# Attention pairs 0 to 12 on 64-row TensorE tiles, in a new order, with q and k stacked and one division for both heads

## The chip, the cores and the metric

The kernel runs on one core of a Trainium2 chip. The core has a matrix engine (TensorE, PE), whose results land in PSUM, a memory of eight banks; VectorE (DVE), ScalarE (ACT) and GpSimd (POOL), which compute on PSUM and on SBUF, the working memory of 128 partitions; and SyncE (SP), which issues transfers. Each engine takes its own instructions in the order in which they are written and waits for others by semaphores. The metric is device time in microseconds, the median of several runs. Smaller is better.

## The reference

Attention with a bias that depends on the distance of two positions, for 8 batches of 8 heads of 576 positions and 64 channels; then a layer of two matrix products with a leaky rectifier between them.

```python
scores = scale * np.matmul(q, k.transpose(0, 1, 3, 2))
bias = bias_table[bucket]                  # bucket from |i - j|; one value for |i - j| >= 128
scores = scores + bias.transpose(2, 0, 1)[None, :, :, :]
attn = np.exp(scores - np.max(scores, axis=-1, keepdims=True))
attn = attn / (np.sum(attn, axis=-1, keepdims=True) + 1e-09)
x = np.matmul(attn, v)                     # heads side by side: (4608, 512)
h = x @ w_in                               # (512, 2048)
out = np.maximum(0.01 * h, h) @ w_out      # (2048, 512)
```

## The kernel before

The work is 32 pairs of heads (`items`: batch b, pair p, numbered n = 4b + p), interleaved with pieces of the layer. All matrix operands are bf16.

**A pair.** Its rows of q and k come from DRAM in blocks that lie on `RQ` = 96 partitions, six positions to a partition (`load_qk`, L119; tiles `qn`, `kn`). They have to be turned, so that the 64 channels of each of the two heads lie on partitions: `turned_pair` (L280) does it on TensorE for pairs 0 to 8, by identity products into PSUM tiles `ps_t` (for pairs 0 to 5 straight from the loaded rows, 12 of them for q and 12 for k; for 6 to 8 from rows that `pair_rows`, L265, has put side by side on VectorE, 6 and 6). From pair 9 on a DMA transpose (`turn_by_dma`, L276) does it. Copies then bring q and k into `qt` and `kt` (`copy_q`, `copy_k`). Scores (`qk_mm`, L333) have keys on partitions: four blocks u of 128 keys for the first 512 queries, both heads in one buffer `ps_s` of two banks; u = 4 is the last 64 queries against the four blocks; u = 5 is the last 64 keys of both heads, laid over 128 rows with zeros between (`apart`, L297). `exp` (L370) is the exponential on ScalarE into `at`, `at4`; `band` (L387) multiplies the near-diagonal part by the exponential of the bias (`hk`) on VectorE. The value products add to two banks `ps_o`, one for each head: `av_tails` (L412) for the last keys, then `av_chunks` (L425), `av` or `av_phase` (L465) for the four blocks; a 65th column of ones gives the row sums. `divide` (L447) takes a reciprocal and a product for each head, into `opair`, which is turned once more into `xT`, the layer's input: on TensorE (`x_turn`, L484) or by DMA (`x_transposes`).

**The layer.** For each of nine blocks T of 512 tokens there are 16 "in" pieces (four products of 512 columns into one bank `pm`, then a leaky rectifier on ScalarE, `leaky`, into `gt`) and four "out" pieces of 16 products each, copied to `y` and stored. Block 0 needs all four pairs of batch 0, block 1 those of batches 0 and 1.

**Tile height.** A product may use all 128 rows of TensorE, or 64: two with different halves of the rows then run at the same time. Scores use 64 rows a head (L354). Before, the value products of pairs 0 to 6 (`av_chunks`, L432) and of pair 31 (`av`, L442) use 128 rows, and so do most layer pieces ahead of pair 13 (L532, L584); the rest of that stretch goes by halves of the rows (L476, L720). From pair 13 on (`body_in_lanes`, L915) everything goes in two 64-row lanes (`lanes`, L849): each layer piece is done in two halves, and two pieces run side by side. Two halves must not add to the same bank at the same time; where that could come about, `hold` (L460) puts an empty TensorE instruction that waits for the end of a given product.

**What sets the order.** Pairs 0 to 7 follow a list written out by hand (`first`, L1115; `m n u` is a score, `e` its exponential, `b` a bias product, `at` and `ac` value products, `dv` a division, `i`, `p0`, `p1`, `moe` and `o` layer pieces). Pairs 8 to 12 follow a loop (L1213) with a plan of layer pieces (`plan`, `body_in_halves`, L739); pairs 13 to 31 `body_in_lanes`; then `moe_rest` (L1023). PSUM is split into two `ps_s` buffers of two banks, two single banks `ps_o`, and two single banks that `ps_t`, `ps_tx` and `pm` share. GpSimd issues the loads in the order of `load_qk`, `load_v_part` and `spread_loads` (L1075); SP the stores and DMA transposes.

Of the kernel before, what the change touches and what calls it, by code (L numbers as in the profile page):

```python
# [37 lines left out]
def kernel(  # L38
# [10 lines left out]
    nc = tc.nc  # L49
# [23 lines left out]
    op_pool = ctx.enter_context(tc.tile_pool(name="op", bufs=2))  # L73
# [20 lines left out]
    RQ = 96  # L94
    NC = S // RQ
    qn = [per.tile([P, H, NC, D], BF16, name=f"qn{i}") for i in range(NBUF)]
    kn = [per.tile([P, H, NC, D], BF16, name=f"kn{i}") for i in range(NBUF)]
# [21 lines left out]
    def load_qk(b, h0, h1, which=("q", "k")):  # L119
        i = b % NBUF  # L120
        for name, src, dst in (("q", q, qn[i]), ("k", k, kn[i])):
            if name not in which:
                continue
            nc.gpsimd.dma_start(
                out=dst[0:RQ, h0:h1, :, :].rearrange("r h c d -> r h (c d)"),
                in_=src[b, h0:h1, :, :].rearrange("h (r c) d -> r h (c d)", c=NC),
            )
# [148 lines left out]
    def turn_by_dma(n):  # L276
        t = turned[n] = tu_pool.tile([P, 2 * NC, RQ], BF16, name="tu")
        nc.sync.dma_start_transpose(out=t, in_=prs.pop(n).rearrange("r j c d -> r (j c d)"))

    def turned_pair(n, j):  # L280

        if by_dma(n):
            return turned[n][:, j * NC : (j + 1) * NC, :].rearrange("p c r -> p r c")
        ps = ps_m_pool.tile([P, 8 * P], BF16, name="ps_t", tag="m")
        b, p = items[n]
        for c in range(NC):
            if n > n_pairs + 1:
                nc.tensor.transpose(ps[:, c * RQ : (c + 1) * RQ], in_=prs[n][:, j, c, :],
                                    identity=ident[0:RQ, 0:RQ])
                continue  # L290
            for e in range(2):
                nc.tensor.transpose(ps[e * D : (e + 1) * D, c * RQ : (c + 1) * RQ],  # L292
                                    in_=(qn, kn)[j][b % NBUF][0:RQ, 2 * p + e, c, :],
                                    identity=ident[0:RQ, 0:RQ])
# [1040 lines left out]
```

## Time and profile before

| what | value |
|---|---|
| median of 3 runs | 364.85 us (364.39 to 365.44) |
| profiled execution, first to last instruction (its span) | 362.8 us |
| TensorE busy in it | 353.4 us (97%) |
| VectorE busy | 189.5 us (52%) |
| ScalarE busy | 243.4 us (67%) |
| GpSimd busy | 107.4 us (30%) |
| mean granted TensorE clock | 0.995 |

The profile is one execution. It gives no time of its own for what lies around the span; the median of the runs is 2.1 us over the span. An engine's busy time is the union of its instructions. A row of the timeline gives start, length, engine, source line, operation, `out<-in`, the tile of TensorE (rows*columns), shapes and a count; a length over several instructions runs from the first start to the last end, and products overlap, since each lasts longer than the distance to the next. What stands in brackets at a row's end is idle time before it and what ended it.

### The profile page before, as it was taken

The page shows a single profiled execution, that of the slowest core. Times are in us where ns is not written, and L with a number is a line of the kernel's source. Part 1 is how long each engine was busy: PE and PEld are TensorE (multiplying, and loading weights), DVE is VectorE, ACT ScalarE, POOL GpSimd, SP SyncE. Part 2 cuts the span into 40 slices and gives each one's busy share as a digit, 9 for nine tenths or more (in the row PEclk, how much of TensorE's full clock was granted, in tenths as well). Part 3 has the DMA queues.
Part 4 walks back from the last instruction along what each step waited for, and adds up shares of the span by engine and source line. Part 5 has one row for each costly group of instructions (what it writes and reads, how often), then busy time and mean ns, then how long its engine had stood idle before and what let it go on. Part 6 is the DMA issues. An engine that isn't in the chain of part 4 may idle for free.

```text
span 362.8 us, 12074 instructions
## 1 busy us (share of the span) xinstructions
PE 353.4 (97%) x5174; PEld 204.7 (56%) x5191; DVE 189.5 (52%) x499; ACT 243.4 (67%) x364; POOL 107.4 (30%) x195
## 2 busy tenths in 40 slices
PE   7899999999999999999999999999999999999996
PEld 3465555555556777666666665565666544444443
DVE  3796876677756767655555566556554300200000
ACT  5999888479958898777777777777776264054111
POOL 8857617254334344432243334211000000000000
PEclk8999999999999999999999999999999999999999
DMA  8999999997899899979998889875111000210212
GB/s 104 196 193 147 190 206 159 197 156 115 99 130 137 114 148 139 138 120 122 133 136 124 108 119 129 122 103 96 52 49 51 29 31 0 85 33 0 80 66 87
DMA packets 106429, 40.27 MB, mean 111 GB/s; under 512 B 83713, under 2 KB 102409, under 8 KB 106377
## 3 DMA queue, kind: packets, MB, share of 16 engines
q0 software_dynamic: 55200, 18.36, 48.4%
q1 hardware_dynamic: 49880, 19.06, 27.2%
q10 hardware_dynamic: 1296, 2.10, 1.6%
q8 instruction: 41, 0.67, 0.7%
q14 instruction: 12, 0.09, 0.1%
HBM read 37.68 MB, written 9.45 MB: 130 GB/s over the span
## 4 chain that ended last, share of the span: by engine, by line
PE 93%; DVE 3%; ACT 1%; issue 1%; DMA 1%; POOL 0%; ACTq 0%; POOLq 0%
PE pm L845 35%; PE pm L584 16%; PE pm L532 15%; PE ps_o L476 8%; PE ps_s L354 8%; PE pm L720 2%; PE ps_o L432 2%; PE ps_o L421 1%; PE ps_s L845 1%; DMA kn<-in_k_dram 1%; DVE at L408 1%; PE ps_t L292 1%; PE pm L577 1%; PE ps_s L347 1%; PE ps_s L357 1%
## 5 line engine op out<-in xcount | busy, mean ns | idle before, releaser
L845 PE MATMUL pm<-xT,w_in_sb 64*128 64x512 bf16 x608 | 142.1, 376 | 0.0
L373 ACT ACTIVATE at<-ps_s 128x1024 bf16<-128x1024 f32 x120 | 118.6, 1026 | 33.7 <-PE ps_s L354 32.1
L845 PE MATMUL pm<-w_out_sb,gt 64*128 64x512 bf16 x544 | 132.6, 376 | 0.0
L556 ACT ACTIVATE gt<-pm 128x512 bf16<-128x512 f32 x140 | 82.1, 605 | 38.8 <-PE pm L532 33.4
L408 DVE TENSOR_TENSOR at<-at,hk 128x768 bf16<-128x768 bf16 (+3 forms) x149 | 65.6, 453 | 41.6 <-ACT at L385 24.8
L845 PEld LDWEIGHTS <-w_in_sb 64*128 64x128 bf16 x608 | 50.7, 94 | 20.4 <-issue 0.7
L845 PEld LDWEIGHTS <-gt 64*128 64x128 bf16 x544 | 47.0, 94 | 22.7 <-issue 3.5
L584 PE MATMUL pm<-w_out_sb,gt 128*128 128x512 bf16 x261 | 59.0, 379 | 0.7 <-issue 0.5
L532 PE MATMUL pm<-xT,w_in_sb 128*128 128x512 bf16 x242 | 56.9, 379 | 0.5
L354 PE MATMUL ps_s<-qt,kt 64*128 64x512 bf16 x240 | 44.3, 383 | 2.3 <-ACT at L373 0.8
L584 PEld LDWEIGHTS <-gt 128*128 128x128 bf16 x268 | 25.5, 98 | 29.9
L532 PEld LDWEIGHTS <-w_in_sb 128*128 128x128 bf16 x252 | 23.7, 98 | 27.0 <-issue 0.6
L476 PE MATMUL ps_o<-vn,at 64*128 64x65 bf16 x1920 | 38.4, 190 | 0.0
L476 PEld LDWEIGHTS <-at 64*128 64x128 bf16 x1920 | 35.7, 94 | 4.6 <-issue 4.4
L131 POOL DMA_DIRECT2D vn<-in_v_dram x32 | 33.8, 1060 | 9.1 <-issue 4.2
L385 ACT ACTIVATE at<-ps_s 128x576 bf16<-128x576 f32 x30 | 19.9, 663 | 17.9 <-PE pm L845 17.9
L454 DVE TENSOR_TENSOR opair<-ps_o,rcp 128x320 bf16<-128x320 f32 x64 | 29.1, 487 | 1.1
L896 DVE COPY y<-pm 128x512 f32<-128x512 f32 x17 | 11.8, 692 | 27.7 <-PE pm L845 27.7
L597 DVE COPY y<-pm 128x512 f32<-128x512 f32 x11 | 7.6, 691 | 33.5 <-PE pm L584 30.6
L354 PEld LDWEIGHTS <-kt 64*128 64x128 bf16 x240 | 14.7, 94 | 16.7 <-issue 6.6
L1088 POOL COPY tick<-opair 1x1 bf16<-1x1 bf16 x43 | 7.9, 185 | 54.6 <-DVE opair L454 54.6
L1088 POOL COPY tick<-at 1x1 bf16<-1x1 bf16 x21 | 5.5, 263 | 61.0 <-DVE at L408 61.0
(108 smaller groups left out, 348.9 us busy)
## 6 DMA issues: line engine op xcount, KB each, us to landing
out_dram<-y SPq DMA_DIRECT2D x24, 256.0 KB, 3.7
qn<-in_q_dram POOLq DMA_DIRECT2D x28, 144.0 KB, 4.7
kn<-in_k_dram POOLq DMA_DIRECT2D x28, 144.0 KB, 3.5
vn<-in_v_dram POOLq DMA_DIRECT2D x24, 128.0 KB, 4.5
w_in_sb<-in_moe_w_in_dram POOLq DMA_DIRECT2D x4, 512.0 KB, 9.2
w_out_sb<-in_moe_w_out_dram POOLq DMA_DIRECT2D x2, 1024.0 KB, 13.4
out_dram<-y ACTq DMA_DIRECT2D x7, 256.0 KB, 2.0
vn<-in_v_dram POOLq DMA_DIRECT2D x16, 64.0 KB, 8.0
```

The source lines that it names most:

```text
L131: nc.gpsimd.dma_start(out=vn[b % NBUF][:, c, h0:h1, 0:D], in_=v[b, h0:h1, c * P : (c + 1) * P, :].rearrange("h s d -> s h d"),)
L354: nc.tensor.matmul(ps[:, e, :], lhsT=kt[r, u * P : (u + 1) * P], rhs=qt[r, 0:512], start=True, stop=True)
L373: nc.scalar.activation(at[:, :, u, 0:512], ps, AF.Exp, scale=scale)
L385: nc.scalar.activation(at4[:, 0:w], ps.rearrange("p e i -> p (e i)")[:, 0:w], AF.Exp, scale=scale)
L408: nc.vector.tensor_tensor(out=o, in0=o, in1=m, op=ALU.mult)
L454: nc.vector.tensor_tensor(out=opair[:, 0:m, e * D : (e + 1) * D], in0=ps[:, :, 0:D], in1=rcp.to_broadcast([P, m, D]), op=ALU.mult)
L476: m = nc.tensor.matmul(outs[n][e][:, ic * (D + 1) : (ic + 1) * (D + 1)], lhsT=at[halves[r], o : o + P], rhs=vn[b % NBUF][halves[r], c, 2 * ...
L532: nc.tensor.matmul(pm, lhsT=w_in_sb[:, c, f * P : (f + 1) * P], rhs=xT[c][:, T * TT : (T + 1) * TT], start=(c == 0), stop=(c == n_cc - 1))
L556: nc.scalar.activation(g, pm, AF.Prelu, bias=0.0, scale=1.0, alpha=0.01)
L584: nc.tensor.matmul(pm, lhsT=gt[:, f, ts * P : (ts + 1) * P], rhs=w_out_sb[:, f, :], start=(f == 0), stop=(f == n_fc - 1))
L845: m = nc.tensor.matmul(o, lhsT=w, rhs=x, start=was is None, stop=need[bank] == 0)
L1088: nc.gpsimd.tensor_copy(out=tick, in_=at4_[home(n)][0:1, S - 1 : S] if part == 2 else ops_[n - 2 + part][0:1, 0, 0:1])
```

## The change

Five things are changed together.

1. `RQ` is 64. q lies on partitions 0 to 63 and k on 64 to 127 of one tile `qkn`, nine positions to a partition. `pair_rows` makes one copy for both, the DMA transpose turns nine blocks of 128 rows instead of twelve of 96, and `turn_by_pe` turns q and k with 64-column products on the two halves of the rows. Pair 9 keeps the DMA, pairs 0 to 8 TensorE.
2. The value products of all pairs go in two lanes (`value_steps`), as do the last-key scores (`Tails`: two half-width products of each lane) and the output transposes (`x_turn`, two halves); the layer pieces of the first part come as `Duo`, two pieces side by side.
3. `ps_o` is one buffer of two banks. `divide` makes one reciprocal and one product for both heads. A `Duo` in a two-bank buffer is closed by one rectifier of 1024 columns.
4. A new list orders pairs 0 to 12 (before: 0 to 7, then the loop). The planner and `body_in_halves` are gone; pairs 13 to 31 keep `body_in_lanes`, where two pieces `i2`, `i3` now share the `ps_o` buffer, and the next pair's first score comes behind the last pieces. The three warming products (`warm`) are gone.
5. The last pair's value products are woven with four layer pieces; `moe_rest` follows with five banks in turn instead of six.

```diff
-    RQ = 96
+    RQ = P // 2
...
+    qkn = [per.tile([P, H, NC, D], BF16, name=f"qkn{i}") for i in range(NBUF)]
+    rows_of = {"q": slice(0, RQ), "k": slice(RQ, P)}
...
-        t = prs[n] = pr_pool.tile([RQ, 2, NC, 2 * D], BF16, name="pr")
-        for j, src in enumerate((qn, kn)):
-            nc.vector.tensor_copy(out=t[:, j, :, :].rearrange("r c (e d) -> r c e d", e=2),
-                                  in_=src[b % NBUF][0:RQ, 2 * p : 2 * p + 2, :, :].rearrange("r e c d -> r c e d"))
+        t = prs[n] = pr_pool.tile([P, NC, 2 * D], BF16, name="pr")
+        nc.vector.tensor_copy(out=t.rearrange("r c (e d) -> r c e d", e=2),
+                              in_=qkn[b % NBUF][:, 2 * p : 2 * p + 2, :, :].rearrange("r e c d -> r c e d"))
...
+    def turn_by_pe(n, which):
...
+        for c in range(NC):
+            for j in which:
+                r = halves[j]
+                o = ps[j][:, c * RQ : (c + 1) * RQ]
+                if rows is not None:
+                    nc.tensor.transpose(o, in_=rows[r, c, :], identity=ident[r, r])
+                    continue
+                for e in range(2):
+                    nc.tensor.transpose(o[e * D : (e + 1) * D, :], in_=qkn[b % NBUF][r, 2 * p + e, c, :],
+                                        identity=ident[r, r])
...
+            for e in range(2):
+                need[id(ps), e] = 2
+                t.append(((id(ps), e), ps[:, e, 0:w], kt[:, S : S + P], qt[:, e * w : (e + 1) * w]))
+            self.todo = [[t[0], t[1]], [t[1], t[0]]]
...
+    def divide(n):
+        ops_[n] = op_pool.tile([P, NJ + 1, 2 * D], BF16, name="opair")
+        of = outs.pop(n)[:, :, 0 : (NJ + 1) * (D + 1)].rearrange("p e (i d) -> p e i d", d=D + 1)
+        rcp = rc_pool.tile([P, 2, NJ + 1, 1], FP32, name="rcp")
+        nc.vector.reciprocal(rcp, of[:, :, :, D : D + 1])
+        nc.vector.tensor_tensor(out=ops_[n].rearrange("p i (e d) -> p e i d", e=2), in0=of[:, :, :, 0:D],
+                                in1=rcp.to_broadcast([P, 2, NJ + 1, D]), op=ALU.mult)
...
+        def go(self, i, k):
+            a, b = self.p
+            if i:
+                a, b = b, a
+            lanes(a.take(0, k), b.take(1, k))
...
+                nc.scalar.activation(g, self.both, AF.Prelu, bias=0.0, scale=1.0, alpha=0.01)
...
-        i2, i3 = Piece("in", ps_o_pool, "o0"), Piece("in", ps_o_pool, "o1")
+        i23 = Duo("in", "o")
+        i2, i3 = i23.p
...
+            lanes(i2.take(0, 4) + i3.take(0, 4), two.take(1, 8))
+            i23.close()
+            lanes(i4.take(0, 4), two.take(1, 4))
+            i4.close()
+            two.close(True)
             if nxt:
                 score(n + 1, 0)
-            for i in (i2, i3, i4):
-                lanes(i.take(0, 4), two.take(1, 4))
-                i.close()
-            two.close(True)
             return
...
-            chunks = {(n_pairs + 2, 2): (0,), (n_pairs + 3, 1): (1, 2, 3)}.get((n, part), ())
+        if n <= 3 * n_pairs:
+            chunks = {(6, 2): (0, 1, 2, 3), (9, 1): (0, 1), (10, 1): (2, 3)}.get((n, part), ())
...
-        ac 3 1 3, e 4 2, p0 0,
-        begin 4, m 4 3, dv 3 0.1, e 4 3, xt 3 o0, xc 3, b 4 0, p0 1, p1 0 0, p1 1 0, m 4 4 s, b 4 1, m 4 5,
+        l t5 0 1 t5 1 1, x1 2, l t5 0 1 t5 1 1, xc 2 v, x0 3, e 5 5, m 5 0, b 4 1, x1 3, e 5 0, m 5 2, xc 3 v,
+        b 5 5, sl 5 2, in f0F1 m, d f0F1 0 2, b 4 5, e 5 2, at 4, b 5 0, m 5 4, d f0F1 0 2, e 5 4, m 4 4, b 5 2,
```

The order of the engines is best seen where the layer begins. On TensorE, before, its first products (`pm`, three of piece 0) stand ahead of pair 4's score of block 3 and pair 3's output transposes:

```order
L532 LDWEIGHTS w_in_sb
L532 MATMUL pm_791<-xT_94,w_in_sb 128x512
L532 LDWEIGHTS w_in_sb
L532 MATMUL pm_791<-xT_95,w_in_sb 128x512
L532 LDWEIGHTS w_in_sb
L532 MATMUL pm_791<-xT_96,w_in_sb 128x512
L354 LDWEIGHTS kt_111
L354 MATMUL ps_s<-qt_118,kt_111 128x512
L354 LDWEIGHTS kt_111
L354 MATMUL ps_s<-qt_118,kt_111 128x512
L490 LDWEIGHTS opair
L490 MATMUL ps_tx<-ident,opair 128x128
```

In the changed kernel they come behind pair 5's score of block 2 (L341), two pieces (`pm_1094`, `pm_1096`) in turn on the two halves:

```order
L341 LDWEIGHTS gt
L341 MATMUL ps_s<-gt 128x512
L341 LDWEIGHTS gt
L341 MATMUL ps_s<-gt 128x512
L406 LDWEIGHTS w_in_sb
L406 MATMUL pm_1094<-xT_94,w_in_sb 128x512
L406 LDWEIGHTS w_in_sb
L406 MATMUL pm_1096<-xT_94,w_in_sb 128x512
L406 LDWEIGHTS w_in_sb
L406 MATMUL pm_1094<-xT_95,w_in_sb 128x512
L406 LDWEIGHTS w_in_sb
L406 MATMUL pm_1096<-xT_95,w_in_sb 128x512
```

The start of the layer has moved from ahead of a score of pair 4 to behind one of pair 5, and 128-row and 64-row products no longer alternate.

On ScalarE, before, the last rows ahead of the first rectifier (L556) are pair 3's and pair 4's exponentials and two copies of turned q (L307):

```order
L373 ACTIVATE at_112<-ps_s 128x2x512 x3
L307 COPY qt_118<-ps_t 128x576
L385 ACTIVATE at_0_114<-ps_s 128x576
L375 ACTIVATE at_112<-ps_s 128x8x64
L307 COPY gt<-ps_t 128x576
L373 ACTIVATE at_113<-ps_s 128x2x512 x4
L556 ACTIVATE gt<-pm_791 128x512
```

In the changed kernel the same stretch ahead of the first rectifier (L546) holds pair 4 and most of pair 5, and one copy of turned k (L316):

```order
L356 ACTIVATE at_111<-ps_s 128x2x512 x3
L316 COPY gt<-ps_t 128x576
L362 ACTIVATE at_1_113<-ps_s 128x576
L356 ACTIVATE at_111<-ps_s 128x2x512
L362 ACTIVATE gt<-ps_s 128x576
L356 ACTIVATE gt<-ps_s 128x2x512 x2
L358 ACTIVATE gt<-ps_s 128x8x64
L358 ACTIVATE at_111<-ps_s 128x8x64
L356 ACTIVATE gt<-ps_s 128x2x512
L546 ACTIVATE gt<-pm_1094 128x512
```

Seven exponentials more than before precede the layer's first rectifier, and copies of q have gone to VectorE.

On VectorE, around pair 3's outputs, before, the reciprocals and divisions come in twos:

```order
L452 RECIPROCAL rcp<-ps_o 128x5 x2
L454 TENSOR_TENSOR opair<-ps_o,rcp 128x5x64 x2
L496 COPY xT_97<-ps_tx 128x576
L408 TENSOR_TENSOR at_113<-at_113,hk 128x2x256
L408 TENSOR_TENSOR at_113<-at_113,hk 128x2x384
```

In the changed kernel one of each does for both heads, and pair 2's and pair 3's output copies follow close together:

```order
L470 RECIPROCAL rcp<-ps_o 128x10
L471 TENSOR_TENSOR opair<-ps_o,rcp 128x2x5x64
L502 COPY xT_96<-ps_tx 128x576
L386 TENSOR_TENSOR at_111<-at_111,hk 128x2x384
L502 COPY xT_97<-ps_tx 128x576
```

Two instructions a pair are gone, and a bias product of pair 4 stands between the two output copies.

More of the change, by code (lines that the diff above doesn't have):

```diff
@@ L463, in hold @@
         tc.add_manual_dep(f.ins, sooner.ins.name, ended, reason="the other rows have left this bank")
[L465 to L479 removed]
+    wrote, need, kept, outs = {}, {}, [], {}
@@ new lines, with product, lanes @@
+    order = {"made": 0, "ended": 0}
+    def product(bank, o, w, x, r):
+        was = wrote.get(bank)
+        if was is not None and was[0] != r and was[2] > order["ended"]:
+            hold(was[1])
+            order["ended"] = was[2]
+        need[bank] -= 1
+        m = nc.tensor.matmul(o, lhsT=w, rhs=x, start=was is None, stop=need[bank] == 0)
+        order["made"] += 1
+        wrote[bank] = (r, m, order["made"])
+    def lanes(*two):
+        at = [0, 0]
+        todo = [list(x) for x in two]
+        while todo[0] or todo[1]:
+            r = 0 if todo[0] and (at[0] <= at[1] or not todo[1]) else 1
+            bank, o, w, x = todo[r].pop(0)
+            product(bank, o, w[halves[r]], x[halves[r]], r)
+            at[r] += x.shape[-1]
@@ new lines, in x_turn @@
+    def x_turn(n, r, ps=None):
+        if r == 0:
+            ps = ps_m_pool.tile([P, 8 * P], BF16, name="ps_tx", tag="m")
+        h = halves[r]
+        last = wrote.get(("x", n))
+        if last is not None and last[2] > order["ended"]:
+            hold(last[1])
+            order["ended"] = last[2]
+        for ic in range(NJ + 1 - r):
+            m = nc.tensor.transpose(ps[:, ic * P + r * SL : ic * P + (r + 1) * SL],
+                                    in_=ops_[n][h, ic, :], identity=ident[h, h])
+        order["made"] += 1
+        wrote["x", n] = (r, m, order["made"])
@@ L711, in side_by_side @@
-    def side_by_side(one, two):
-        def phase(k, lo, hi, last=None):
-            if last is not None:
-                hold(last)
-            for c in range(lo, hi):
-                for r in range(2):
-                    pm, steps, low = one if r == k else two
-                    w, x = steps[c]
-                    m = nc.tensor.matmul(pm, lhsT=w[halves[r]], rhs=x[halves[r]], start=(k == 0 and c == 0),
-                                         stop=(low is not None and k == 1 and c == n_cc - 1))
-            return m
-        return phase
@@ L835 @@
-    wrote, need, kept = {}, {}, []
-    order = {"made": 0, "ended": 0}
-    def product(bank, o, w, x, r):
-        was = wrote.get(bank)
-        if was is not None and was[0] != r and was[2] > order["ended"]:
-            hold(was[1])
-            order["ended"] = was[2]
-        need[bank] -= 1
-        m = nc.tensor.matmul(o, lhsT=w, rhs=x, start=was is None, stop=need[bank] == 0)
-        order["made"] += 1
-        wrote[bank] = (r, m, order["made"])
-    def lanes(*two):
-        at = [0, 0]
-        todo = [list(x) for x in two]
-        while todo[0] or todo[1]:
-            r = 0 if todo[0] and (at[0] <= at[1] or not todo[1]) else 1
-            bank, o, w, x = todo[r].pop(0)
-            product(bank, o, w[halves[r]], x[halves[r]], r)
-            at[r] += x.shape[-1]
@@ L1304 @@
+    lanes(d.take(0, 1), c.take(1, 1))
+    lanes(b.take(0, 4), a.take(1, 4))
+    a.close()
+    b.close()
+    lanes(d.take(0, 3), c.take(1, 3))
+    d.close()
+    c.close()
+    x_copy(n, x_turn(n, 1, x_turn(n, 0)))
+    for m in range(N):
+        finished(m)
+    while stores:
+        o, y = stores.pop(0)
+        nc.sync.dma_start(out=o, in_=y)
+    rest["on"] = True
+    for _ in range(4):
+        piece_out()
     moe_rest()
```

824 lines of the change are left out of this document (254 added, 570 removed).

## The prediction

> **What bounds the kernel now.** I read the page first (busy time of each engine, the 40 slices), then a table by stage, then the timelines of TensorE, ScalarE and VectorE around the first product of the second layer.
>
> ```profile
> span 362.8 us, 12074 instructions
> ...
> PE 353.4 (97%) x5174; PEld 204.7 (56%) x5191; DVE 189.5 (52%) x499; ACT 243.4 (67%) x364; POOL 107.4 (30%) x195
> ```
>
> TensorE is busy 97% of the span, but that is an average over stages. The next rows cut the span at the first input of the transposes, at the first product of the layer (w_in, L532), at the last score of pair 13, and at TensorE's last product; the columns are window: length, then busy us of PE, PEld, DVE, ACT, POOL, each with its count, then the granted clock.
>
> ```profile
> 5.37:31.16 25.79, 22.27 (x429) 14.89 (x430) 19.02 (x51) 23.38 (x32) 18.32 (x29) 0.93 1.40 182
> 31.16:114.83 83.67, 82.84 (x1231) 45.44 (x1239) 61.30 (x157) 63.98 (x98) 38.61 (x66) 1.00 1.21 155
> 114.83:359.94 245.11, 244.68 (x3507) 143.13 (x3512) 106.84 (x271) 153.40 (x227) 46.30 (x90) 1.00 0.58 90
> 359.94:362.79 2.85, 0.00 (x0) 0.00 (x0) 0.00 (x0) 0.27 (x1) 0.00 (x0) 1.00 0.28 92
> ```
>
> Call them A, B, C and the tail. In A there is nothing but attention, and ScalarE (23.38 of 25.79 us) is the tightest engine, VectorE behind it. In B and C TensorE has the layer's products to fill with and stands still 0.83 and 0.43 us: whatever TensorE is spared in B is time saved; what it is spared in A is not, unless ScalarE and VectorE get there sooner. By the two program orders, 234 full products' worth of the layer has been done at the end of B before and after, so B's end is the same point of the work and C holds the same work.
>
> The second thing to see is what TensorE pays when it goes between products of 128 rows (two heads or a whole K chunk) and of 64 rows.
>
> ```profile
> 34.71 1.89 PE L532 MATMUL pm<-xT,w_in_sb 128*128 128x512 bf16 x8
> 36.53 0.39 PE L354 MATMUL ps_s<-gt 64*128 64x512 bf16 x2
> 36.76 0.32 PE L421 MATMUL ps_o<-v,at 64*128 64x65 bf16 x10
> 36.91 0.38 PE L354 MATMUL ps_s<-gt 64*128 64x512 bf16 x2
> 37.22 0.79 PE L432 MATMUL ps_o<-vn,at 128*128 128x65 bf16 x20
> ```
>
> Eight products of 512 columns take 1.89, of which the last alone is 0.38: one each (1.89 - 0.38) / 7 = 0.216. The ninth should start at 34.71 + 8 x 0.216 = 36.44 and starts at 36.53; the pair of 36.91 ends its turn at 37.13 and the 128-row products start at 37.22. A change of tile height costs 0.09 to 0.10 us each way; two 64-row products on different halves cost as much together as one of 128 rows.
>
> **The change, part by part.** *Tile height.* Counted in the program orders, TensorE changes height 30 times in A, 33 in B, once in C; the changed kernel once at the start and once before its last stretch. B is spared 33 x 0.096 = 3.2 us. A's 30 (2.9 us) lie under ScalarE and are not counted.
>
> *Turning q and k.* Before, 12 transposes of 96 columns make one of q or k.
>
> ```profile
> 17.99 0.45 PE L292 MATMUL ps_t<-ident,qn 96*64 96x96 bf16 x12
> 18.37 0.33 PE L432 MATMUL ps_o<-vn,at 128*128 128x65 bf16 x5
> ```
>
> That is 18.37 - 17.99 = 0.38 us a dozen. B has one dozen and six half dozens, about 1.9 us; after, 27 pairs of 64-column transposes side by side. No row shows one; bounds are 0.015 (the spacing of single 65-column products below, four quarters at once) and 0.06 a pair (nothing side by side). I take one 65-column pair, 0.0305, so 0.8 us: saved 1.1, between 0.3 and 1.5.
>
> *The rest of B by the same kind of count* (0.216 for 512 columns full or as a pair, 0.0305 for a 65-column pair):
>
> ```profile
> 149.57 0.61 PE ps_o L476 x40
> ...
> 159.06 0.61 PE ps_o L476 x40
> ```
>
> 0.61 / 20 = 0.0305; the 128-row kind is (0.79 - 0.19) / 19 = 0.032. Before: layer 234 x 0.216 = 50.5; values 120 x 0.032 + 285 x 0.0305 = 12.5; scores 37 pairs and 40 pairs of 64 columns 9.2; last key rows 9 x 0.245 = 2.2; q and k 1.9; output transposes 1.1; height 3.2. Sum 80.6 of the 83.67 that B lasts. What is left over, 3.1 us, is the 0.83 of idleness and 2.2 that I put on the 12 places where TensorE waits for its own other half (the empty instruction of `hold`): up to 0.18 each. After: 50.5, values 405 x 0.0305 = 12.4, scores 34 pairs and 40 small 8.5, last rows 14 x 0.122 = 1.7, q and k 0.8, outputs 0.6. Sum 74.5. The scores and last rows that leave B (1.2 us) are now done in A, where TensorE has time.
>
> *Holds.* After, B has 42. Their price is unknown between 0 (the 64-row pairs of C come every 159.06 - 149.57 = 9.49 us, and the same count of their work, 32 x 0.216 + 45 x 0.0305 + 1.2, is 9.5: seven holds in each cost nothing that shows) and 0.18. In the new order something else mostly stands between the two halves, as in C, so I take 0.04: 1.7 us, at most 7.6. With 0.8 us of idleness kept, B lasts 74.5 + 0.8 + 1.7 = 77.0 instead of 83.7.
>
> *Where A ends.* The first layer product waits for pair 3's outputs and, in the new order, stands behind a score of pair 5 that needs the buffer of pair 5's last-row exponential. ScalarE has 30 exponentials and one copy to do until then; before, 25 and four copies stood there. Their spacing:
>
> ```profile
> 7.42 2.85 ACT L373 ACTIVATE at<-ps_s 128x1024 bf16<-128x1024 f32 x3 [0.67 <-PE ps_s L354]
> ...
> 24.21 2.85 ACT L373 ACTIVATE at<-ps_s 128x1024 bf16<-128x1024 f32 x3
> 26.94 0.66 ACT L307 COPY qt<-ps_t 128x576 bf16<-128x576 bf16 x1
> 27.46 0.69 ACT L385 ACTIVATE at<-ps_s 128x576 bf16<-128x576 f32 x1
> 28.00 0.64 ACT L375 ACTIVATE at<-ps_s 128x512 bf16<-128x512 f32 x1
> 28.48 0.69 ACT L307 COPY gt<-ps_t 128x576 bf16<-128x576 bf16 x1
> ```
>
> (26.94 - 24.21) / 3 = 0.91 for 1024 columns, 0.54 for 576, 0.48 for 512, 0.52 for a copy. So 20 x 0.91 + 6 x 0.54 + 4 x 0.48 + 0.52 = 23.9 us from the first exponential, which I put at 7.2 (q and k are turned as early, q first): 31.1, and 31.4 with the score behind it. VectorE has its own chain from the arrival of the bias rows to the copy of pair 3's output:
>
> ```profile
> 13.15 0.54 DVE L401 TENSOR_TENSOR at<-at,hk 64x192 bf16<-64x192 bf16 x2 [1.61 <-DMA hk<-u_row]
> ...
> 20.07 0.75 DVE L313 COPY kt<-ps_t 128x576 bf16<-128x576 bf16 x1
> 20.74 0.42 DVE L408 TENSOR_TENSOR gt<-gt,hk 128x512 bf16<-128x512 bf16 x1
> 21.07 0.22 DVE L299 TENSOR_TENSOR kt<-kt,own 128x128 bf16<-128x128 bf16 x1
> 21.21 0.55 DVE L408 TENSOR_TENSOR gt<-gt,hk 128x768 bf16<-128x768 bf16 x1
> 21.68 0.20 DVE L452 RECIPROCAL rcp<-ps_o 128x5 f32<-128x5 f32 x1
> 21.91 0.49 DVE L454 TENSOR_TENSOR opair<-ps_o,rcp 128x320 bf16<-128x320 f32 x1
> 22.32 0.45 DVE L496 COPY xT<-ps_tx 128x576 bf16<-128x576 bf16 x1
> 22.68 0.55 DVE L408 TENSOR_TENSOR gt<-gt,hk 128x768 bf16<-128x768 bf16 x1
> ...
> 23.78 0.25 DVE L408 TENSOR_TENSOR gt<-gt,hk 128x192 bf16<-128x192 bf16 x1
> 24.19 0.49 DVE L408 TENSOR_TENSOR gt<-gt,hk 128x640 bf16<-128x640 bf16 x1 [0.16 <-ACT gt L375]
> 24.60 0.75 DVE L313 COPY kt<-ps_t 128x576 bf16<-128x576 bf16 x1
> ...
> 32.65 0.46 DVE L496 COPY xT<-ps_tx 128x576 bf16<-128x576 bf16 x1 [0.55 <-PE ps_tx L490]
> ```
>
> From start to start: turned copy 0.67, bias products 0.33, 0.47 and 0.41 (512, 768 and 640 columns), 0.17 for 192 (0.25 less the 0.08 by which neighbours overlap), mask 0.14, reciprocal 0.23, division 0.41, output copy 0.36. One division for both heads has 640 columns and no row: a copy of 512 columns from the same memory
>
> ```profile
> L896 DVE COPY y<-pm 128x512 f32<-128x512 f32 x17 | 11.8, 692 | 27.7 <-PE pm L845 27.7
> ```
>
> is the nearest, 0.69, and two divisions, 0.82, are the upper end; I take 0.75, so 0.98 a pair with its reciprocal instead of 1.28. In the new order 44 instructions stand from the first bias product to that output copy: 10 of 768 columns (4.7), 5 of 512 (1.65), 4 of 640 (1.64), 3 of 192 (0.5), the two on half the rows (0.45), 5 turned copies (3.35), 3 masks (0.4), 4 divisions (3.9), 4 output copies (1.45), together 18.1: 13.15 + 18.1 = 31.3. Both chains end together, so neither can be late without the other waiting. Without a gap the layer starts at 31.4; with VectorE as loosely filled as now (its pieces from 13.15 to 32.65 sum to 17.1 of 19.5, 88%) at 33.8. Following the two queues and the two score buffers by these spacings, I find few gaps and take 32.2: 1.0 later than now.
>
> *C and the tail.* The value results now sit in one buffer of two banks, shared with two layer pieces that one 1024-column activation clears. In a pair of C that activation starts 0.2 us behind the second piece (a product of 0.38 outlasts its turn of 0.216 by 0.16) and takes 2.85 - 2 x 0.91 = 1.03; TensorE meanwhile has four more pairs and two scores, 0.86 + 0.43. That is even, so I add 0.3 us over all of C, and the score that is moved behind the last pieces costs nothing as long as that holds. C's end and the tail are kept.
>
> *At nothing.* One row copy for q and k together instead of two, fewer and longer pieces in the loads and in the turning by DMA, values of the next batch fetched at other places of the GpSimd queue: these lie beside TensorE, with VectorE at 61.30 of B's 83.67 us and 106.84 of C's 245.11. The one new place where they can show is pair 9, which is now turned by DMA in the middle of B.
>
> ```profile
> tu<-pr SPq DMA_TRANSPOSE x23, 4.1
> ```
>
> Issue to landing is 4.1 us; between the request and the copies that wait for it TensorE has nine groups of layer products of 0.43, three of 0.86, two scores and an output transpose, about 7.2 us. Behind those copies VectorE holds the bias products of pair 8; were the 4.1 doubled, 1.0 us would show.
>
> **Sum.** A +1.0, B -6.7, C +0.3: -5.4 on a span of 362.8. The median of the runs, 364.85, stands 2.1 us over the span, and I move it by the same amount: **359.5 us**.
>
> **Rivals.** *A, later still.* The gaps come in, 33.8 or more; or the clock drops.
>
> ```profile
> 3.41:6.87 3.46, 1.77 (x31) 1.00 1.08 141
> 6.87:10.28 3.41, 3.41 (x40) 0.50 1.50 167
> 13.69:17.10 3.41, 2.22 (x38) 1.00 1.27 233
> ```
>
> TensorE ran one stretch of 3.41 us at half clock, right after a stretch with 1.77 us of work; 2.22 did not bring it about. In A the changed kernel has some 3 us less for TensorE (2.9 of height changes, 0.9 of transposes and the three warming products of L1155, 0.3; 1.2 of scores more), so a second half-clock stretch may come: it would cost up to 3.41 / 2 = 1.7 us. Either gives 361 to 363.5. The Trainium skill, page "TensorE: Matmul & The Clock Gate", section "Why this matters for your kernels", has the clock fall only after a gap of over some 3 us. By that rule A has no second stretch and the sum stays at 359.5, where the rows above allow 361.2; the trace speaks against the rule, since TensorE worked 1.77 us in the stretch before the half clock.
>
> *The holds give it back.* At 0.15 to 0.18 each, 42 cost 6.3 to 7.6 instead of 1.7: 364.1 to 365.4, no change to speak of. For it: the 2.2 us left over in B; against: C.
>
> *Slower: the single two-bank buffer.* In C the cover above is even, and behind it VectorE has a bias product (waiting for the moved score's exponential), a turned copy and then the division that frees the same buffer. If the activation finds ScalarE at another 0.91 us piece, each pair waits about that long. C has 18 pairs: from 5.4 / 18 = 0.3 us a pair on the gain is gone, and at 0.45 the time is 367.6.
>
> **How the numbers follow.** Forecast, 356.5 to 361.5: 0.68. A later: 0.12. Holds give it back: 0.08. Buffer, slower: 0.12. The low end is holds at nothing (-1.7), the layer at 31.4 (-0.8) and idleness halved (-0.4). The high end takes in A later and the start of the hold rival, 363.8. A measurement of this kernel tells 0.3%, 1.1 us, from no change: faster 0.80, same 0.08, slower 0.12.
>
> **What would show it.** Right: no 128-row products between the start and the last stretch; the first layer product between 31.4 and 33.8; the end of B near 109; pairs of C still 9.5 us apart. Wrong: waits of value products for activations in C, spacing over 9.7, or TensorE idle over 3 us in B.

## The result: slower, and the profile after

| | before | changed |
|---|---|---|
| median of 4 runs | 364.69 us | 378.47 us |
| lowest to highest | 364.39 to 365.44 | 376.19 to 382.02 |
| ratio | 1 | 1.0356 (95%: 1.0319 to 1.0393) |
| span of the profiled execution | 362.8 us | 374.4 us |

The ratio, here and below, leaves out runs more than 1.5% above the fastest of their kernel; without the run of 382.02 us the changed kernel's median is 377.74.

359.5 us was predicted, with faster as the likely sign; the kernel is 3.6% slower, and its executions lie much further apart than those before. The page of the changed kernel has these lines in place of those shown of before (TensorE 97%, 12,074 instructions):

```profile
span 374.4 us, 13307 instructions
...
PE 356.6 (95%) x5856; PEld 222.4 (59%) x5856; DVE 177.3 (47%) x394; ACT 246.8 (66%) x336; POOL 99.6 (27%) x192
...
PE   7867689999999999999999999999999999999996
...
PEclk9689999999999999999999999999999999999999
...
PE 92%; issue 3%; ACT 3%; DVE 1%; ACTq 0%
```

The last line is the chain of the work that ended last, followed back from the end, as shares of the span by engine. Before it read

```profile
PE 93%; DVE 3%; ACT 1%; issue 1%; DMA 1%; POOL 0%; ACTq 0%; POOLq 0%
```

so "issue" has grown from 1 to 3%. TensorE is busy 90% or more from the seventh slice on (56 us) up to the last one; nearly all its idleness stands in front. The table by stage, cut at the same places as before (first layer product, the product behind the first score of pair 14, last product; the columns are those of the prediction), says how much:

```profile
5.40:37.55 32.15, 24.33 (x695) 15.48 (x696) 23.00 (x53) 26.25 (x33) 23.00 (x36) 0.84 1.36 176
37.55:125.28 87.73, 81.56 (x1564) 48.70 (x1560) 47.62 (x102) 66.31 (x87) 29.27 (x56) 1.00 1.10 137
125.28:371.55 246.27, 246.08 (x3575) 156.47 (x3572) 104.13 (x218) 151.56 (x209) 43.04 (x90) 1.00 0.56 89
371.55:374.40 2.85, 0.00 (x0) 0.00 (x0) 0.00 (x0) 0.27 (x1) 0.00 (x0) 1.00 0.27 92
```

Against the forecast, A ends 5.35 us late (37.55, not 32.2), B lasts 10.7 longer (87.73, not 77.0), and C 0.9 (246.27, not 245.4; 245.11 before). That is 17.0, the whole distance between the 357.4 that the sum gave for the span and 374.4. (The end of B, called the last score of pair 13 in the prediction, is the first score of pair 14; 114.83 is the right row for it.)

What stands in A and B that was not there before is seen in the waits of TensorE from 5 to 75 us (engine, output, line, what was waited for: us in all, times, longest) and in the pieces over 0.5 us that the chain of waits has there (start, length):

```profile
PE ps_o L406 <- issue: 7.4, 6, 2.0
PE ps_tx L493 <- issue: 2.1, 1, 2.1
PE ps_s L341 <- ACT at L356: 0.9, 3, 0.4
```

```profile
20.73 2.06 issue
28.57 0.66 issue
32.44 1.06 issue
38.54 1.07 issue
44.64 1.96 issue
51.46 1.47 issue
64.88 1.19 issue
```

"Issue" means that TensorE waited for nothing that the profile knows: no semaphore, no data, no engine. 9.5 us in seven stalls, while the largest named cause, the exponentials on ScalarE, has 0.9. What the stalls have in common is not a line or a tile but a distance. From the end of one to the end of the next TensorE does this:

```profile
22.78:29.23 6.45, 5.11 (x127) 3.05 (x126) 4.21 (x10) 4.97 (x7) 3.95 (x6) 0.74 1.50 195
29.23:33.49 4.26, 2.97 (x127) 2.06 (x127) 3.56 (x9) 3.77 (x5) 3.51 (x6) 1.00 1.16 97
33.49:39.60 6.11, 4.76 (x125) 2.94 (x126) 4.23 (x11) 4.40 (x6) 5.05 (x7) 1.00 1.22 194
39.60:46.59 6.99, 4.99 (x127) 3.28 (x126) 3.15 (x7) 4.60 (x7) 2.35 (x5) 1.00 1.51 187
46.59:52.92 6.33, 4.87 (x126) 3.15 (x127) 3.02 (x6) 5.08 (x7) 1.07 (x4) 1.00 1.23 207
```

Products plus weight loads (PE and PEld) are 253, 254, 251, 253 and 253; with the few empty instructions of `hold`, which the columns leave out, each stretch holds exactly 256 instructions (the seventh stall stands 512 behind the sixth). The view of transfers shows what arrives in such portions. From 31 to 67 us the changed kernel has

```profile
q0 software_dynamic: 12278, 5.85, 141.6%
...
q8 instruction: 6, 0.10, 1.1%
```

(queue: packets, MB, share), where the kernel before has

```profile
q0 software_dynamic: 12859, 5.71, 133.8%
...
q8 instruction: 3, 0.05, 0.5%
```

Six packets of instructions, 16 KB each, instead of three, past much the same loads (5.85 and 5.71 MB). In the whole run queue q8 has 46 packets, for TensorE's 11,875 records: one packet for 256. Row by row (instruction number on TensorE, when the block before it began, when its packet was on its way, when TensorE went on, and its idle time before that):

```
block from   block before began   packet            goes on   idle
   705           16.56            20.24 to 21.13     22.79    2.1
  1473           33.50            37.27 to 38.22     39.61    1.1
  1729           39.61            44.15 to 45.09     46.59    2.0
  1985           46.59            50.56 to 51.62     52.93    1.5
  5313          135.06           136.21 to 137.14   142.56    none
```

While the loads run, a packet starts 3.7 us (median of 10, up to 4.5) behind the start of the block before, instead of 1.0 (median of 31) from 80 to 290 us; it takes 0.9 to 1.2, and TensorE goes on 1.3 to 1.7 behind its end. So there a block usually costs about 6.2 us (3.7 + 1.0 + 1.5, an estimate), however little work is in it. Pairs of 64-row products do the work of one 128-row product with twice the instructions: 40 such products in 0.61 us use up 80.

The Trainium skill, page "Runtime: NRT & Kernel Launch", section "Instruction fetch mechanics", has instructions come in blocks of 16 KiB, 256 of them, and calls the cost of the boundary mostly hidden. The packets agree; hidden it was in this trace at every boundary behind 80 us, but not at seven of the ten between 16 and 71 us.

### The profile page after: what moved, and what is told of

Same layout as the page of the kernel before. It is cut to its first block, busy times and chain, and to the rows that moved or that the text cites. A ratio compares the mean times of both kernels' runs of the same rounds, so it can differ in the third digit from the quotient of the medians.

```text
span 374.4 us, 13307 instructions
## 1 busy us (share of the span) xinstructions
PE 356.6 (95%) x5856; PEld 222.4 (59%) x5856; DVE 177.3 (47%) x394; ACT 246.8 (66%) x336; POOL 99.6 (27%) x192
## 4 chain that ended last, share of the span: by engine, by line
PE 92%; issue 3%; ACT 3%; DVE 1%; ACTq 0%
PE pm L406 35%; PE ps_o L406 23%; PE pm L574 11%; PE ps_s L341 8%; PE pm L529 7%; PE ps_s L406 5%; ACT at L356 1%; PE ps_w L789 1%; PE pm L567 1%; DVE opair L471 1%; PE ps_tx L493 1%; ACT at L358 0%; PE ps_t L292 0%; ACT at L362 0%; ACT gt L683 0%
## 5 line engine op out<-in xcount | busy, mean ns | idle before, releaser
L406 PE MATMUL pm<-w_out_sb,gt 64*128 64x512 bf16 x736 | 158.0, 376 | 0.0
L356 ACT ACTIVATE at<-ps_s 128x1024 bf16<-128x1024 f32 x118 | 116.0, 1029 | 12.8 <-PE ps_s L341 11.6
L406 PE MATMUL pm<-xT,w_in_sb 64*128 64x512 bf16 x432 | 100.2, 376 | 0.0
L406 PE MATMUL ps_o<-xT,w_in_sb 64*128 64x512 bf16 x368 | 82.3, 376 | 0.1
L546 ACT ACTIVATE gt<-pm 128x512 bf16<-128x512 f32 x86 | 50.4, 598 | 30.3 <-PE pm L529 25.8
L406 PEld LDWEIGHTS <-at 64*128 64x128 bf16 x2700 | 56.5, 95 | 22.0 <-issue 12.7
L341 PE MATMUL ps_s<-qt,kt 64*128 64x512 bf16 (+1 forms) x468 | 51.7, 290 | 2.0 <-ACT at L356 0.6
L362 ACT ACTIVATE at<-ps_s 128x576 bf16<-128x576 f32 x30 | 19.6, 652 | 26.0 <-PE pm L406 17.9
L341 PEld LDWEIGHTS <-kt 64*128 64x128 bf16 x480 | 25.3, 94 | 16.6 <-issue 5.7
L829 POOL COPY tick<-opair 1x1 bf16<-1x1 bf16 x40 | 11.2, 280 | 83.7 <-DVE opair L471 83.7
L683 ACT ACTIVATE gt<-ps_o 128x1024 bf16<-128x1024 f32 x23 | 23.6, 1025 | 14.9 <-PE ps_o L406 14.8
L529 PE MATMUL pm<-xT,w_in_sb 128*128 128x512 bf16 x128 | 28.0, 379 | 0.0
L471 DVE TENSOR_TENSOR opair<-ps_o,rcp 128x640 bf16<-128x640 f32 x32 | 26.4, 825 | 1.3
L406 PE MATMUL ps_s<-qt,kt 64*128 64x288 bf16 x120 | 22.3, 289 | 0.8 <-ACT at L362 0.3
```

The lines of the kernel that those rows point to most:

```text
L341: nc.tensor.matmul(o, lhsT=kt[r, j * P : (j + 1) * P], rhs=qt[r, i], start=True, stop=True)
L356: nc.scalar.activation(at[:, :, u, 0:512], ps, AF.Exp, scale=scale)
L362: nc.scalar.activation(at4[:, 0:S].rearrange("p (h i) -> p h i", h=2), ps[:, :, 0 : S // 2], AF.Exp, scale=scale)
L406: m = nc.tensor.matmul(o, lhsT=w, rhs=x, start=was is None, stop=need[bank] == 0)
L471: nc.vector.tensor_tensor(out=ops_[n].rearrange("p i (e d) -> p e i d", e=2), in0=of[:, :, :, 0:D], in1=rcp.to_broadcast([P, 2, NJ + 1, D] ...
L529: nc.tensor.matmul(pm, lhsT=w_in_sb[:, c, f * P : (f + 1) * P], rhs=xT[c][:, T * TT : (T + 1) * TT], start=(c == 0), stop=(c == n_cc - 1))
```

## Experiments

The main theory ("supply"): TensorE uses up its instructions faster than they come while the loads run. The rivals: half clock ("clock"; the granted clock was 0.5 from 11.34 to 18.17 and from 24.99 to 28.41, where the kernel before has 6.87 to 10.28), the new order itself ("order"), the waits for the other half (holds). Times are medians of four runs (eleven where said); before stood at 364.6 to 365.1 beside them. "Stalls" are waits over 0.3 us at a 256th instruction.

**Fewer instructions.** In the changed kernel, for pairs 0 to 7:

```diff
     def av_phase(n, phase, chunks=range(NJ)):
+        if n < WHOLE:
+            return av_whole(n, phase, chunks)
         lanes(*value_steps(n, phase, chunks))
+
+    WHOLE = 8
...
+                m = nc.tensor.matmul(outs[n][:, e, ic * (D + 1) : (ic + 1) * (D + 1)], lhsT=at[:, i : i + P],
+                                     rhs=vn[b % NBUF][:, c, 2 * p + e, :], start=False, stop=need[key] == 0)
```

> The changed kernel, with the values of pairs 0 to 7 on 128 rows again, in the same order. Supply theory (TensorE stands still because its instructions, which arrive 256 at a time, are used up faster than they come while the loads run): 640 of the 2,750 instructions that TensorE has had by 70.5 us go, two and a half packets; TensorE's waits for nothing the profile shows fall from 9.5 us (5 to 75 us) to under 4, the first layer product comes from 37.7 to 34 to 35.5, and although some 60 height changes of 0.1 come back, the time is 367 to 372. Clock theory (what is lost is TensorE at half clock): the half-clock stretches stay, time 375 to 379. Order theory (the new order of the first pairs is slow by itself): 376 to 382, by the height changes rather slower than the changed kernel.

371.97 us, 1.0195 (1.0165 to 1.0225). Where 9.5 us of unnamed waits stood from 5 to 75 us, 0.3 is left; one stall of 0.8 comes at 106. The first layer product comes at 34.75, and stretch B is

```profile
34.75:119.90 85.15, 83.60 (x1404) 47.79 (x1400) 47.37 (x102) 66.41 (x87) 31.97 (x60) 1.00 1.19 149
```

2.6 shorter, though 30 height changes (2.9 us) are back in it. Supply holds; 5.8 us are won against 377.74, and 7.3 against the kernel before are not.

**Fewer loads.** `load_w_in` and `load_w_out` become `nc.gpsimd.memset(..., 0.01)`; TensorE's instructions stay.

> The changed kernel without the six loads of the layer's weights (the weights are set to 0.01 by GpSimd instead, so the layer's result is another), instructions of TensorE unchanged. Supply theory: the other loads are through by about 40 us, packets of instructions then come as soon as they are asked for (0.4 to 2.5 us after the block before has begun, as behind 80 us, instead of 3.3 to 4.5), and the five stalls behind 37 us (1.07, 1.96, 1.47, 1.19 and what hangs on them) go: waits of 9.5 us fall to 3 to 5, time 368 to 373. Clock and order theories: the stalls have nothing to do with the loads, 375 to 379.

371.04 us, 1.0166 (1.0138 to 1.0194). The stalls from 28 us on go (two of 0.9 and 0.3 at 111 and 116 appear); that of 23 us, when q, k and v still arrive, stays:

```profile
PE ps_tx L490 <- issue: 2.6, 1, 2.6
```

TensorE's program is the same as in the changed kernel; its stalls are 3.9 us in all instead of 9.5, and the profiled span is 369.5 instead of 374.4. Two edits with nothing in common, fewer instructions or fewer loads, take the same stalls of 28 to 67 us away (but for the 0.3 in the first). Supply, as expected.

**The clock.** The scores of pairs 0 to 2 twice, first in the changed kernel, then in that of the first experiment; and in the kernel before (pairs 0 and 1, and two more products at the start):

```diff
-                nc.tensor.matmul(o, lhsT=kt[r, ...], rhs=qt[r, i], start=True, stop=True)
+                for _ in range(2 if n < 3 and u < NJ else 1):
+                    nc.tensor.matmul(o, lhsT=kt[r, ...], rhs=qt[r, i], start=True, stop=True)
```

> The changed kernel, with the score products of pairs 0 to 2 done twice each (12 pairs of 512 columns more, 2.6 us of work for TensorE at places where it waits for ScalarE, 48 instructions more). Clock theory: at most one of the three half-clock stretches is left, 3.4 us of TensorE time come back, time 372 to 375. Supply theory: the waits stay at 9 to 11 us at the same places of the instruction stream, whatever the clock does, time 375 to 380.

> The changed kernel with the values of pairs 0 to 7 on 128 rows (372.0) and the scores of pairs 0 to 2 twice. Here hardly an instruction comes late, so the clock stands alone. Clock theory: the half-clock stretch of 11.0 to 17.9 goes, the first layer product comes at 32.5 to 33.5 instead of 34.75, time 369.5 to 371. If the clock costs nothing there: 372 to 373. Supply theory adds that the 48 instructions may bring one more late packet, up to 1 us.

> The kernel before with two more products of 512 columns at the start and the scores of pairs 0 and 1 done twice (8 pairs of products, 32 instructions). Clock theory (a stretch with little work brings half clock in the next one or two): the half-clock stretch of 6.87 to 10.28 goes, up to 1.7 us are gained, 363 to 364.5. If ScalarE and VectorE set the pace there anyway: 364.5 to 366.

380.95 us (1.0417, 1.0372 to 1.0462), 372.09 (1.0211, 1.0182 to 1.0239), and 365.32 (1.0019, 1.0010 to 1.0027, 11 runs). In the second and third the clock is whole throughout,

```profile
5.37:34.36 28.99, 25.73 (x577) 15.71 (x572) 22.74 (x53) 26.00 (x33) 21.29 (x34) 1.00 1.38 179
```

and nothing is gained: 372.09 against 371.97, and 0.7 us lost by the kernel before. The first lies above both of its forecasts; its profile, of the longest of its four runs (386.40), has 11.3 us of stalls up to 47 us, and half clock from 23.2 to 36.8 and from 43.7 to 50.5. As the main cause the clock falls: the kernel with the values on 128 rows kept a half-clock stretch (11.0 to 17.9) and lost its stalls all the same. A small price is not excluded, since the doubled scores are 2.6 us of work themselves; the first layer product came at 34.36 with them and at 34.75 without.

**More instructions, more loads, in the kernel before.** A product of one column ahead of each early value product, first with one column of weights, then with all 128; and, alone, 24 copies of 512 KB from memory to memory in pairs 15 to 22.

```diff
+                nc.tensor.matmul(outs[n][e][0:1, 400:401], lhsT=at[:, o : o + 1], rhs=vn[...][:, c, 2 * p + e, 0:1], ...)
```

```diff
+                nc.tensor.matmul(outs[n][e][:, 400:401], lhsT=at[:, o : o + P], rhs=vn[...][:, c, 2 * p + e, 0:1], ...)
```

```diff
+        for quarter in range(3):
+            nc.gpsimd.dma_start(out=again.ap()[n - 15, :, o], in_=moe_w_in[:, o])
```

> The kernel before, with one product of 1 column into an unused column ahead of each of the 280 value products on 128 rows of pairs 0 to 6: 560 more instructions in the stretch in which the loads run, about as many as the change adds there, with almost no work in them (up to 0.015 us each, of which the 120 in stretch B show: 1.8). Supply theory: blocks of 256 that lasted 6.2 to 9 us would last 5 to 7, TensorE stands still 2 to 5 us at every 256th instruction, time 367 to 370. Order and clock theories: no waits over 0.5 us that the profile can't name, time 364.5 to 366.5.

> The kernel before with one product of 1 column, with the same 128 weights, ahead of each of the 280 value products on 128 rows of pairs 0 to 6 (into an unused column): 560 more instructions of the same tile shape in the stretch of the loads, 0.01 to 0.03 us of work each, of which the 120 in stretch B show by 1.2 to 3.6 us. Supply theory: blocks of 256 that lasted 6.2 to 9 us would last 5 to 7 and run dry: waits at every 256th instruction, 1 to 4 us together, time 367 to 371. Without it: no waits over 0.5 us that the profile can't name, 366 to 368.5.

> The kernel before with 24 copies of a quarter of w_in from memory to memory (512 KB each, three in each of the pairs 15 to 22) on GpSimd's queue; TensorE's instructions and their order are those of the kernel before. Supply theory: in these pairs (about 125 to 205 us) 256 instructions of TensorE last 4.7 to 8.4 us and now arrive as late as in the early stretch, about 6.2 us after the block before them has begun, so the blocks of 4.7 to 5.3 us stand still: waits that the profile can't name at every 256th instruction, 0.5 to 1.5 us each, together 2 to 5 us where the kernel before has none; time 367 to 370. Any theory by the order, the holds or the clock: no such waits, 364.5 to 366.

The first is no test, and its forecast missed: 450.71 us (1.2361, 1.2317 to 1.2406). Weights of one column are a tile shape of their own, and here, at half clock, a one-column product and the change behind it take 0.10 (30.18 to 30.28):

```profile
30.02 0.23 PE L434 MATMUL ps_o<-vn,at 128*128 128x65 bf16 x1
30.18 0.17 PE L432 MATMUL ps_o<-vn,at 128*1 128x1 bf16 x1
30.28 0.24 PE L434 MATMUL ps_o<-vn,at 128*128 128x65 bf16 x1
```

Its table by stage has TensorE busy without a break and the clock at half:

```profile
40.00:60.00 20.00, 20.00 (x193) 13.01 (x191) 5.90 (x16) 7.93 (x10) 1.34 (x2) 0.50 0.93 141
```

The second, 374.35 (1.0271, 1.0250 to 1.0293), puts two stalls (0.7 and 1.4 us, at 25.0 and 31.5) into a kernel that had none, 256 instructions apart and together in the predicted 1 to 4 us. The time is above the predicted 367 to 371: the other 7.6 of its 9.7 us are the added products in B (0.03 each, 3.7) and the rest of a first layer product that came at 37.0. In the third TensorE's program is that of the kernel before, untouched. 428.53 us (1.1767, 1.1732 to 1.1801), far over the expected 367 to 370, because the values of later batches came late behind the copies; but among the waits are stalls that the kernel before has nowhere:

```profile
PE ps_o L476 <- DMA vn<-in_v_dram: 43.1, 5, 15.2
PE ps_s L354 <- issue: 2.8, 1, 2.8
PE ps_o L476 <- issue: 2.7, 1, 2.7
PE ps_s L347 <- issue: 2.1, 1, 2.1
```

They end at 233.1, 187.6 and 177.6 us, at instructions 6328, 5560 and 5304 of TensorE's records: 768 and 256 apart.

**Where it counts, and cures.** The values on 128 rows in pairs 0 to 2 alone (`WHOLE = 3`); w_out's loads in pairs 6 and 7 instead of 0 and 2; the first experiment's value products in one piece a head; the last two together.

> The changed kernel with the values of pairs 0 to 2 alone on 128 rows: 240 instructions of TensorE fewer before 37 us, where TensorE does not set the pace, and nothing fewer behind. Supply theory: the stalls of 22.8, 29.2 and 33.5 us (3.9 us together) shrink to under 1, those behind 37 us (5.7) stay; the first layer product comes at 34.5 to 35.5, time 374 to 377. If stalls in the attention-only stretch cost nothing: first layer product still near 37.5, 378 to 380.

> The changed kernel with the two loads of w_out (2 MB of the 9.8 MB that GpSimd's queue loads between 5 and 75 us) asked for in pairs 6 and 7 (about 47 and 54 us) instead of at 37 and 42. TensorE's instructions and order unchanged, nothing left out. Supply theory: the load traffic between 38 and 48 us is thinner, the stalls of 39.6 and 46.6 (3.0 us) shrink by half or more, those of 52.9 and 66.1 stay or grow: all waits 7 to 9 us, time 375 to 378. Theories without the loads: no difference to the changed kernel, 377 to 379.

> The kernel of the first experiment (values of pairs 0 to 7 on 128 rows, 372.0) with each head's value products of these pairs in one piece, at the place of the last of them: 34 changes of tile height instead of 62, 28 x 0.1 = 2.8 us of TensorE's work less, about 1.6 of it behind the first layer product. If height changes cost what the trace of before shows: 369.5 to 371. If the pieces of 0.64 us delay scores and so ScalarE: 371.5 to 373.

> The kernel of e11 with the loads of w_out later as in e10: with few late packets left there is little to gain, 0 to 0.7 us less than e11 by the supply theory, no difference without it. Both e11 and e12 stay slower than the kernel before (364.7) by 4 us or more, since what is left is not the supply.

376.58 us (1.0334, 1.0284 to 1.0385): the first layer product comes at 35.2, as expected, so stalls in A do cost there; but 8.9 us of stalls stand behind it, not the expected 5.7. 379.48 (1.0450, 1.0388 to 1.0512), a miss: those of 39.6 and 46.6 shrank by a seventh only (0.9 and 1.7), that of 52.9 shrank to 0.9, that of 66 went, and waits of 1.1 and 1.6 at a 256th instruction came at 69.6 and 106.3 (for the first the profile names ScalarE). The edit moved less than was meant: the two loads were issued at 41.1 and 58.7 us, where the changed kernel has 37.0 and 42.0, so one of them still ran beside the stalls of 46 and 52. 372.06 (1.0207, 1.0163 to 1.0252) lies in the second of its two ranges; 28 height changes fewer won nothing, but the profile has a new stall of 1.6 us at 32 and the layer beginning at 37.5, so the pieces of 0.64 us are not shown as the reason. 377.67 (1.0333, 1.0287 to 1.0380), a miss: with the later w_out a wait for an output that is turned by DMA came in,

```profile
PE ps_s L406 <- DMA xT<-opair: 2.9, 1, 2.9
```

**What is left without the stalls.** From the kernel of the first experiment (371.97): each head of pairs 0 to 3 divided by itself; the layer pieces between pairs 3 and 8 on 128 rows too; no weight loads.

> The kernel of e1 (values of pairs 0 to 7 on 128 rows, 372.0; first layer product at 34.75) with each head of pairs 0 to 3 divided by itself, the first as soon as its values are done. If the one division of 0.83 us behind both heads lengthens the chain that ends at the first layer product (three of them stand in it, each 0.4 longer than the second of two): first layer product 33.5 to 34.2, time 371 to 371.6. If VectorE's throughput decides (the two take 1.28 a pair instead of 1.06): 34.75 to 35.5, 372 to 373.

> The kernel of e1 with the eight pairs of layer pieces that lie between pairs 3 and 8 on 128 rows too: ten waits of TensorE for its own other half fewer, 74 instructions and 64 products fewer, 14 height changes more (1.4 us by 0.1 each). If the waits for the other half cost 0.15 or more each there: 371 to 372 or less. If they cost 0.05 or less: 372.5 to 373.5. If the new order of the first pairs itself is what is slow, it stays 370 to 374 in both.

> The kernel of e1 without the loads of the layer's weights (set to 0.01 instead, so the layer's result is another). If the rest of the loss (7 us against the kernel before) has to do with the loads in any way (late data, late instructions): 366 to 369. If it is the order and the waits between engines: 371 to 372.5, first layer product 34 to 35.

374.60 us (1.0276, 1.0246 to 1.0306) and 375.18 (1.0284, 1.0242 to 1.0326), both above all their ranges, and 371.41 (1.0179, 1.0160 to 1.0197), as expected. Two divisions are 2.6 us worse, with the first layer product at 39.8: the single division is a gain in this order. The layer pieces on 128 rows bring no gain, but a stall of 1.9 us at 33 came in with them, so the price of the ten holds stays unclear. And without the weights almost nothing more is won: what is left is not the weight loads.

## Why the prediction was wrong

**The step that failed** is the sentence under the first rows, "two 64-row products on different halves cost as much together as one of 128 rows", and the two sums built on it, "I take 32.2" for the end of A and "77.0 instead of 83.7" for B. In TensorE's time it is right; in instructions the pair costs twice, and no term of the sum, no bound and no rival had TensorE's instructions as something that must arrive. What the runs showed in its place: 9.5 us of stalls at 256th instructions, 3.8 in A and 5.7 in B. The narrow margin was visible before: the page had a queue "instruction", and a table of its packets against the 256-instruction blocks shows one block of the kernel before (at 27.0 us) beginning some 2 us behind its packet's end, where TensorE stalls at 1.3 to 1.7.

**A second term was mis-sized**: "234 full products' worth of the layer" at the end of B. The trace of before has records of hardly more (102 and 73 whole products and 120 halves, 235 in all), but some records are missing, as the weight loads show, one for each product (window 31.16 to 114.83):

```profile
L532 PE MATMUL pm<-xT,w_in_sb 128*128 128x512 bf16 x102 | 25.4, 379 | 0.3
L532 PEld LDWEIGHTS <-w_in_sb 128*128 128x128 bf16 x106 | 9.6, 98 | 10.5 <-issue 0.6
L584 PE MATMUL pm<-w_out_sb,gt 128*128 128x512 bf16 x73 | 17.2, 379 | 0.5 <-issue 0.5
L584 PEld LDWEIGHTS <-gt 128*128 128x128 bf16 x76 | 6.8, 98 | 7.5
```

With two more loads just ahead of the window that is 184 whole products and, with 120 halves, 244; the changed kernel has 488 halves in B, which is 244 too. Ten products are 2.2 us. So the prediction's 80.6 for B before should have been 82.8, and with 0.83 of idleness nothing is left of the 83.67: the 2.2 "that I put on the 12 places" of `hold` were products. B after would have been 79.2 instead of 77.0, and the forecast 361.7.

**A**, +5.35: three stalls stand in it (2.06, 0.66, 1.06: 3.8 us). In the first experiment, without them, the first layer product comes at 34.75, still 2.55 behind 32.2. So the rival "A, later still" came in as well: no single engine is full there (TensorE 25.3 and ScalarE 26.0 of 29.35 us), and the "few gaps" of the prediction were 2.5 us on ScalarE behind its first exponential, each ended by a product of TensorE. One piece of it was mis-sized: the division for both heads takes 0.82 instead of 0.75 (0.3 for four). By the traces 35 exponentials stand ahead of the first rectifier, and 30 before: five more, not the seven that are given under "The change".

```profile
35.50 0.22 DVE L470 RECIPROCAL rcp<-ps_o 128x10 f32<-128x10 f32 x1 [1.28 <-PE ps_o L406]
35.76 0.82 DVE L471 TENSOR_TENSOR opair<-ps_o,rcp 128x640 bf16<-128x640 f32 x1
```

**B**, +10.7: four stalls, 5.7. Of the other 5.0 the ten products are 2.2. The holds were about as dear as taken: over the two to six products on each side of B's 46 holds the starts come 1.8 to 2.6 us later in all than by the pace of these products, 0.04 to 0.06 each, against 0.04 taken (42 of them, 1.7), so the rival that has the holds give it back did not come in. Many cost nothing, some 0.1 or 0.2. An instance: two score products start at 102.44, and the value products behind a hold not at 102.66 but at 102.77.

```profile
102.44 0.40 PE L341 MATMUL ps_s<-qt,kt 64*128 64x512 bf16 x2
102.77 0.40 PE L406 MATMUL ps_o<-vn,at 64*128 64x65 bf16 x15
```

This is read from the trace; no run took holds away alone. In the kernel of the first experiment B is 85.15 with 2.9 of height changes and 0.8 of stall, so 4.4 over the forecast are left there too, 2.2 of them the ten products. The other 2 us or so of B are not settled.

**C**, +1.2 for 0.3: the value buffer of two banks was no trap. Its rival ("slower: the single two-bank buffer") had the right sign and the wrong mechanism. The activations that clear that buffer follow each other in ScalarE's timeline at the pace of the pairs:

```profile
168.32 1.02 ACT L683 ACTIVATE gt<-ps_o 128x1024 bf16<-128x1024 f32 x1 [0.96 <-PE ps_o L406]
177.85 1.02 ACT L683 ACTIVATE gt<-ps_o 128x1024 bf16<-128x1024 f32 x1 [0.95 <-PE ps_o L406]
187.39 1.02 ACT L683 ACTIVATE gt<-ps_o 128x1024 bf16<-128x1024 f32 x1 [0.95 <-PE ps_o L406]
```

9.53 us a pair, against the 9.49 of before; from 0.3 us a pair on the rival would have decided.

**The half clock** did what its rows allowed (two stretches instead of one), and no run found a price for it. The rule of the Trainium skill's page "TensorE: Matmul & The Clock Gate", section "Why this matters for your kernels", which the prediction cites, does not hold here either: between 1 us and the half clock of 11.34 TensorE has no gap over 0.4 us.

**What stays open.** Of the 13.0 us between 364.69 and 377.74, 5.8 go with the first experiment's 128-row values (372.0 is what is left, itself with 30 height changes in B). By their own length the stalls are more: 9.5 of the 11.6 us between the two profiled spans, which leaves some 2, an estimate that no run reached. Of the first experiment's 7.3, the two spans show 6.3: 3.6 before the first layer product, 1.5 in B and 1.2 in C. The division and the weight loads were tried and are not it, and the clock gave no gain; of the holds only the trace speaks. Which waits of the order it is, is not settled. No version beat the kernel before.

## What to carry to other kernels

Where TensorE's products are short (65 columns here) and large loads are in flight, count instructions as well as time: a rewriting that keeps the time and doubles the instructions can stall at every 256th. Look for waits that the profile cannot name, and divide the number of instructions between two of them by 256. Using the taller tile until the loads were through took the stalls away here; asking for two of the loads later did not. And count work by weight loads as well as by products: ten products missing from the count were 2.2 us of this forecast.

## What the runs showed of the hardware

- Instructions of TensorE came in packets of 16 KB (46 packets for 11,875 records, 256 each), and its unnamed stalls stood a multiple of 256 instructions apart; where TensorE stalled, it went on 2.3 to 2.6 us behind the start of the transfer, and with loads in flight that start came up to 4.5 us behind the start of the block before.
- The granted clock does not follow the busy time of the page: in the run with one-column weights TensorE was busy 20.00 of 20.00 us (40 to 60 us) at a clock of 0.50.
- Weights of one column between weights of 128 cost 0.10 us a change at a granted clock of 0.50 (30.18 to 30.28 in that run); a change of tile height cost 0.09 to 0.10 at full clock.
- The kernel with the stalls scattered more: 376.2 to 382.0 over four runs, where the kernel before has 364.4 to 365.4 and the one without weight loads 369.8 to 371.7. That the stalls cause the scatter was not tested.
- GpSimd has no row in either trace that reads or writes a PSUM tile; of the engines named at the start, only TensorE, VectorE and ScalarE do.
